# A gated recurrence and a two-layer network on one core: wide first products in the opening, two banks for the last halves, and a new order

## The chip, the cores and the metric

The kernel runs on one core of a Trainium2 chip. A core has five engines that work side by side, each on its own list of instructions: TensorE (PE; its weight loads are listed apart as PEld), VectorE (DVE), ScalarE (ACT), GpSimd (POOL) and SyncE (SP), which issues DMAs. The metric is the device time of one execution in microseconds (us). The kernel before takes 181.42 us, the median of three runs (181.39 to 182.42).

## The reference

Inputs are `q`, `k`, `v` and `f_logit`, each of shape (4 batches, 8 heads, 768 steps, 48), and two weight matrices, 384 x 2048 and 2048 x 384, all float32. What is computed:

```python
f = 1.0 / (1.0 + np.exp(-f_logit))
for t in range(S):
    state = f[:, :, t, :, None] * state + np.einsum('bhd,bhe->bhde', k[:, :, t], v[:, :, t])
    y[:, :, t] = np.einsum('bhd,bhde->bhe', q[:, :, t], state)
x = y.transpose(0, 2, 1, 3).reshape(B * S, H * D)
h = x @ w_in
out = (h * (1.0 / (1.0 + np.exp(-h)))) @ w_out
```

The output is 3072 tokens x 384, float32.

## The kernel before, in words

**Tiling.** The 768 steps of each batch are cut into 6 chunks of 128. A (batch, chunk) is a unit; two units make a pair, and there are 12 pairs, numbered 0 to 11. Pairs 0 to 3 (form "T") hold chunks 0 and 1 of one batch; their rows are loaded interleaved, two steps to a partition. Pairs 4 to 11 (form "N") hold one chunk of two batches. A name such as `ki.3.1` is operation `ki` of pair 3, unit 1.

**What is done for a unit.**

- `f`, `k`, `q`, `v`: loads, issued by SP (L241), for a whole pair or (`f.0.0`, `f.0.1`; `v.4.1` and the like) a half of it.
- `E`, `L`: ACT makes exp(-f) (L248) and log(1 + that) (L260, L263).
- `cs`: PE sums the logarithms along the steps with a triangular matrix (L324, L331) and gives the totals (L328, L334).
- `ia`, `a`, `al`: ACT takes exponentials of the sums (L336) and of the totals (L278, L338).
- `ki`, `qg`: DVE or POOL multiply `k` and `q` with these (L341).
- `tq`, `qkc`: PE transposes both (L348) and ACT or DVE copy the result; or `qkD`, a DMA transpose from SP, in place of both. A copy on ACT or DVE is a helper's line, L185 or L187.
- `sc`: PE makes the scores of the chunk (L369 for T, L373 for N), into two PSUM banks; `at`: DVE multiplies them with a mask (L377).
- `vb`: `v` in bf16 (a copy on ACT, DVE or POOL).
- `y`, `yi`: PE makes the output of the recurrence from scores (L285, L389) and from the state before (L385); `d`: PE makes what the chunk adds to the state (L297, L406); `sd`, `su`: DVE or POOL update the state (L410, L420).
- `yc`, then `yT` and `xc`: the output is copied as bf16, transposed by PE (L397) and copied to `xT`; or `yD`, a DMA transpose (L401).

**The two-layer network, by pairs.** `mi.P.j` is the first product for double block j, 0 to 7: 256 of the 2048 hidden columns. It has 2 column blocks x 3 parts of the sum, six matrix products (L271), each with its own weight load; the moving side is `xT` of both units, 256 columns. `mi.P.j.i`, with a third number, does it for unit i alone, with 128 columns and six products again. `si.P.j` (ACT, L276) takes SiLU of both units at once, from the PSUM bank to `hT`. `mo.P.i.h` is a quarter of the second product of a unit (four matrix products of 384 columns, L306); four of them, h = 0 to 3, add up in one PSUM bank. `oc` copies that bank (ACT or DVE), `so` writes it out (SP or POOL, L316 and L318). In pair 11 the second product is cut once more, `mo.11.i.h.half`, each half with 192 columns, and so are `oc` and `so`.

**Weights.** `wi.0` to `wi.3` load a quarter of `w_in` each (two double blocks: `wi.2` holds double blocks 4 and 5), `wo.0` to `wo.3` a quarter of `w_out`. POOL issues them (L216, L219), with a cast to bf16.

**What sets the order.** The order is written out by hand: `PLAN` is one list of words `operation:engine:buffers`. The engine letter is P, A (ACT), V (DVE), G (POOL) or S (SP). Each engine runs its own words in the list's order, and the tile framework adds the waits. The last field is the buffer that the result gets: for PE a PSUM bank 0 to 7, so an operation waits until the bank's last reader is done. `idle.512.n` is n products on zeros (L465). The first four loads of the list are issued ahead of all else. Where ACT goes over from exponentials to SiLU or back, it loads a table (L513).

In before's list the first products of pairs 0 and 1 are all in single units (`mi.0.2.0` ... `mi.1.6.1`), those of pairs 2 to 11 are for both units.

Of the kernel before, what the change touches and what calls it, by code (L numbers as in the profile page):

```python
# [41 lines left out]
tq.1.0:P:2 q.3.0:S:3 a.2.0:A:3 qg.1.1:G: sc.0.0:P:3,4 qkc.1.0:A:1 sc.0.1:P:6,7 at.0.0.1:V:0 k.3.0:S:3 wi.1:G: at.0.0.0:V: E.3.0:A:1 idle.512.2::5
tq.1.1:P:5 at.0.1.0:V:1 wi.2:G: d.1:P:1,4 qkc.1.1:A: v.2.0:S:2 su.1.0:V:0 wi.0:G: at.0.1.1:V: al.2:A:2 L.3.0:A:0 idle.512.3::2 sc.1.0:P:2,3 ki.2.0:G:4
sc.1.1:P:6,1 at.1.0.1:V:2 vb.0.0:A:2 cs.3.1:P:5 vb.0.1:A:3 at.1.1.0:V:3 qg.2.0:G: al.3:A:3 ia.2.1:A:2 d.0:P:7,3 at.1.1.1:V: a.2.1:A:0 cs.3.0:P:6
ia.3.1:A:4 su.0.0:V:0 qg.2.1:G:2 y.0:P:0,1 a.3.0:A:1 at.1.0.0:V: yc.0.0:A:0 yi.0.1:P: tq.2.0:P:7 a.3.1:A:3 wi.3:G: yc.0.1:V:1 ia.3.0:A:0 y.1:P:0,2
# [4 lines left out]
mi.0.1.1:P:0 si.0.3:A:1 mi.0.1.0:P: mi.0.5.1:P: si.1.5:A: ki.3.0:G: mi.0.0.0:P:6 si.0.1:A: mi.0.6.0:P:5 mi.0.0.1:P: su.1.1:G:0 mi.0.7.1:P:4 si.0.0:A:  # L50
mi.0.7.0:P: si.0.2:A: mi.0.6.1:P: ki.3.1:G: mi.1.1.0:P: si.0.6:A: mi.1.7.0:P:0 tq.3.0:P:6 mi.1.7.1:P: qkc.3.0:A:1 mi.0.4.0:P:2 tq.3.1:P:5 si.1.7:A:
mi.0.4.1:P: f.4.0:S:1 mo.0.0.0:P:6 qkc.3.1:A: mo.0.1.0:P:0 si.1.1:A: mi.1.6.1:P:5 si.0.5:A: mi.1.6.0:P: si.1.2:A: mo.1.1.0:P:7 si.1.6:A: mo.0.1.1:P:
si.0.4:A: si.0.7:A: sc.3.1:P:3,1 sc.3.0:P:5,2 at.3.1.0:V:2 vb.2.0:A:4 mo.0.1.2:P: at.3.1.1:V: mo.1.1.1:P: at.3.0.0:V:3 mo.0.0.1:P: q.4.0:S:4
mo.0.1.3:P: vb.3.0:V:5 mo.1.1.2:P: vb.3.1:V:6 oc.0.1:V:0 mo.1.1.3:P: at.3.0.1:V: v.5.0:S:4 mo.0.0.2:P: vb.2.1:V:2 v.5.1:S: oc.1.1:V:1 d.2:P:4,3
so.1.1:G: y.2:P:1,5 su.2.0:V:0 v.4.0:S:5 d.3:P:0,2 E.4.0:A:0 sd.2.1:V:0 y.3:P:7,4 yc.3.0:V:1 yi.2.1:P: mo.1.0.0:P:3 L.4.0:A:1 yc.2.1:V:2 yT.3.0:P:7
su.3.0:V:0 mo.1.0.1:P: yc.2.0:V:0 v.8.1:S:0 mo.0.0.3:P: sd.3.1:V:1 yT.2.1:P:5 oc.0.0:A:2 cs.4.0:P:0 k.4.0:S:4 xc.2.1:V:2 yi.3.1:P: a.4.0:A:2 so.0.0:G:
mo.1.0.2:P: ia.4.0:A:1 q.4.1:S: xc.3.0:A:3 yT.2.0:P:1 mo.1.0.3:P: xc.2.0:V: E.5.0:A:1 k.6.1:S:5 mi.2.2:P:2 al.4.0:A:4 cs.4.1:P:6 mi.2.3:P:5 al.4.1:A:5
a.4.1:A:3 q.5.0:S:5 L.5.0:A:2 mi.2.7:P:7 k.5.1:S:0 yc.3.1:A:1 mi.2.4:P:1 ia.4.1:A:0 ki.4.0:G:1 q.5.1:S: mi.2.5:P:0 oc.1.0:A:3 vb.4.0:G:3 yT.3.1:P:4
mi.2.0:P:6 xc.3.1:V: su.2.1:G:0 mi.3.6:P:3 si.2.3:A:2 mi.3.1:P:4 qg.4.0:V: si.2.7:A: k.4.1:S: su.3.1:G:0 si.2.5:A: mi.3.7:P:5 si.3.1:A:3 f.6.0:S:2
mi.2.6:P:7 vb.5.1:A:0 si.3.7:A: d.4.0:P:0 v.4.1:S: mi.2.1:P:4 sd.4.0:V:0 si.2.6:A: qg.4.1:V:2 tq.4.0:P:5 si.2.4:A: mi.3.2:P:0 si.2.1:A: k.7.0:S:1  # L60
si.2.0:A: mi.3.0:P:7 ki.4.1:G: qkc.4.0:A:0 cs.5.1:P:1 mi.3.5:P:4 qkD.4.1:S:1 si.3.0:A: mo.2.1.0:P:6 si.2.2:A: si.3.5:A: sc.4.0:P:5,7 v.7.0:S:1
# [485 lines left out]
```

## Time and profile before

| | us |
|---|---|
| median of three runs | 181.42 |
| the profiled execution | 180.93 |
| its span, first to last instruction | 179.2 |
| PE busy | 170.5 |
| PE weight loads busy | 129.0 |
| ACT busy | 132.7 |
| DVE busy | 79.7 |
| POOL busy | 61.6 |

The profiled execution took 180.93 us, of which 179.2 lie between its first and its last instruction. The granted TensorE clock was full in all 40 slices of the page. A row of a timeline reads: start, length, engine, line and operation, output <- inputs, how many, and in brackets the idle time of the engine ahead of it with what ended it. In the chain of waits a row has start, length, and what the time went to. A row of the list of waits has the instruction, what it waited for, the total in us, how often, and the longest. Matrix products overlap, so that the length of one row is longer than what it adds to the next row's start.

### The profile page before, as it was taken

To read this page: it belongs to the slowest core of one execution; us is meant where nothing else is said; L and a number is where in the kernel's file an instruction comes from. 1 tells how busy PE (TensorE), PEld (TensorE's weight loads), DVE (VectorE), ACT (ScalarE), POOL (GpSimd) and SP (SyncE) were. 2 spreads that over 40 slices of the span, in tenths; PEclk is the share of its full clock that TensorE was granted. 3 is DMA by queue.
4 is the path that set the end of the run, shared out by engine and by line. 5 is a ranking of instruction groups with operands and counts; after the bars stand their busy time and mean duration, and the time that the engine had idled before them with its cause. 6 is when DMAs were issued, how large, how long until landed. Compare 5 with 4: busy or idle time off the path is not lost.

```text
span 179.2 us, 4981 instructions
## 1 busy us (share of the span) xinstructions
PE 170.5 (95%) x2042; PEld 129.0 (72%) x2044; DVE 79.7 (44%) x166; ACT 132.7 (74%) x251; POOL 61.6 (34%) x106
## 2 busy tenths in 40 slices
PE   6769989999999999999999999999999999999993
PEld 2345779975788866778678877875876786788782
DVE  7078994008821246456673703342335747500002
ACT  3989983895289999999967558988796991178410
POOL 6036995000274004554044170636303592000010
PEclk9999999999999999999999999999999999999999
DMA  6999999999999799998478998994994496320043
GB/s 159 324 325 325 240 204 207 199 187 190 242 230 212 92 208 221 168 241 144 84 145 170 188 210 141 252 263 103 179 251 94 97 190 215 88 70 0 0 150 117
DMA packets 109366, 31.91 MB, mean 178 GB/s; under 512 B 103536, under 2 KB 108768, under 8 KB 109344
## 3 DMA queue, kind: packets, MB, share of 16 engines
q1 hardware_dynamic: 104464, 25.60, 70.2%
q0 software_dynamic: 4880, 6.00, 15.7%
q8 instruction: 16, 0.26, 0.6%
q14 instruction: 6, 0.05, 0.1%
HBM read 25.17 MB, written 4.72 MB: 167 GB/s over the span
## 4 chain that ended last, share of the span: by engine, by line
PE 77%; ACT 9%; DVE 4%; DMA 3%; SPq 2%; issue 1%; POOL 1%; DVEq 0%
PE pb L306 32%; PE pb L271 32%; ACT hT L276 4%; DMA q<-in_q_dram 3%; PE pb L373 2%; SPq L241 2%; PE pb L385 2%; PE pb L348 2%; PE pb L389 2%; DVE qk L341 2%; ACT L513 1%; DVE atm L377 1%; PE pb L331 1%; PE pb L397 1%; DVE st L420 1%
## 5 line engine op out<-in xcount | busy, mean ns | idle before, releaser
L306 PE MATMUL pb<-w_out_sb,hT 128*128 128x384 bf16 (+1 forms) x416 | 70.4, 314 | 0.2 <-ACT hT L276 0.2
L271 PE MATMUL pb<-xT,w_in_sb 128*128 128x256 bf16 (+1 forms) x672 | 68.9, 257 | 0.0
L271 PEld LDWEIGHTS <-w_in_sb 128*128 128x128 bf16 x672 | 56.6, 98 | 7.5 <-issue 0.3
L276 ACT ACTIVATE hT<-pb 128x512 bf16<-128x512 f32 x96 | 51.8, 617 | 12.4 <-PE pb L271 12.0
L306 PEld LDWEIGHTS <-hT 128*128 128x128 bf16 x416 | 37.7, 98 | 18.7 <-ACT hT L276 0.4
L377 DVE TENSOR_TENSOR atm<-pb,triu 128x512 bf16<-128x512 f32 x32 | 20.6, 684 | 20.5 <-PE pb L373 17.8
L336 ACT ACTIVATE x<-pb 128x384 f32<-128x384 f32 x48 | 22.1, 508 | 1.5 <-PE pb L331 1.4
L420 POOL TENSOR_TENSOR st<-sd,al 48x192 bf16<-48x192 f32 x32 | 16.6, 518 | 18.7 <-PE pb L385 12.1
L341 POOL TENSOR_TENSOR qk<-q,x 128x384 bf16<-128x384 f32 x11 | 11.3, 1025 | 31.9 <-ACT x L336 14.5
L513 ACT ACT_TABLE_LOAD x15 | 19.2, 1283 | 0.3
L185 ACT COPY ob<-pb 128x384 f32<-128x384 f32 (+1 forms) x15 | 6.8, 453 | 12.6 <-PE pb L306 12.6
L377 DVE TENSOR_TENSOR atm<-pb,mask 128x512 bf16<-128x512 f32 x16 | 10.2, 685 | 12.4 <-ACT hT L276 11.1
L187 DVE COPY ob<-pb 128x384 f32<-128x384 f32 (+1 forms) x11 | 5.8, 535 | 22.2 <-PE pb L306 22.2
L318 POOL DMA_DIRECT2D out_dram<-ob x8 | 4.6, 578 | 28.4 <-ACT ob L185 24.8
L316 POOL DMA_DIRECT2D out_dram<-ob x14 | 7.6, 548 | 19.6 <-DVE ob L187 15.9
L341 DVE TENSOR_TENSOR qk<-q,x 128x384 bf16<-128x384 f32 x13 | 7.6, 593 | 13.7 <-ACT x L336 13.7
L248 ACT ACTIVATE e<-f 128x768 f32<-128x768 f32 (+1 forms) x13 | 10.4, 800 | 4.4 <-DMA f<-in_f_logit_dram 4.2
L410 DVE TENSOR_TENSOR sd<-pb,st 128x384 f32<-128x384 f32 x16 | 8.9, 554 | 10.6 <-PE pb L406 3.9
L341 POOL TENSOR_TENSOR qk<-k,x 128x384 bf16<-128x384 f32 x10 | 10.8, 1082 | 6.4 <-ACT al L278 2.0
L185 ACT CAST yb<-pb 128x384 bf16<-128x384 f32 x12 | 5.6, 479 | 9.7 <-PE pb L389 9.6
L341 DVE TENSOR_TENSOR qk<-k,x 128x384 bf16<-128x384 f32 x14 | 9.9, 710 | 0.9 <-ACT x L336 0.9
L187 DVE CAST yb<-pb 128x384 bf16<-128x384 f32 x12 | 6.6, 556 | 8.0 <-PE pb L389 5.9
(72 smaller groups left out, 157.4 us busy)
## 6 DMA issues: line engine op xcount, KB each, us to landing
f<-in_f_logit_dram SPq DMA_DIRECT2D x11, 384.0 KB, 4.7
q<-in_q_dram SPq DMA_DIRECT2D x16, 192.0 KB, 4.1
v<-in_v_dram SPq DMA_DIRECT2D x16, 192.0 KB, 3.9
k<-in_k_dram SPq DMA_DIRECT2D x16, 192.0 KB, 3.9
k<-in_k_dram SPq DMA_DIRECT2D x4, 384.0 KB, 4.8
v<-in_v_dram SPq DMA_DIRECT2D x4, 384.0 KB, 9.5
q<-in_q_dram SPq DMA_DIRECT2D x4, 384.0 KB, 4.9
w_in_sb<-in_moe_w_in_dram POOLq DMA_DIRECT2D x4, 384.0 KB, 9.5
```

The costliest lines, as they stand in the source:

```text
L185: nc.scalar.copy(dst, src)
L187: ENG[eng].tensor_copy(dst, src)
L248: return nc.scalar.activation(e, at("f", P)[:, j * w:(j + 1) * w], AF.Exp, scale=-1.0)
L271: nc.tensor.matmul(h[:, i, cols], w_in_sb[:, kk, n * 128:(n + 1) * 128], at("xT", P)[:, kk, cols], start=(kk == 0), stop=(kk == KT - 1))
L276: return nc.scalar.activation(at("hT", P)[:, 2 * j:2 * j + 2, :], at("h", P, j).rearrange("p (n c) -> p n c", n=2), AF.Silu)
L306: nc.tensor.matmul(at("o", P, i)[:, cols], at("hT", P)[:, n, i * C:(i + 1) * C], w_out_sb[:, n, cols], start=(n == 0), stop=(n == NT - 1))
L336: nc.scalar.activation(at(kind, P, i).rearrange("p h d -> p (h d)"), at("cs", P, i)[:, 0:HD], AF.Exp, scale=1.0 if kind == "ia" else -1.0)
L341: ENG[eng].tensor_mul(at("qk", P, i)[:, j, :, 0:D], heads("qk"[j], P, i), at("ia" if j else "a", P, i))
L377: ENG[eng].tensor_mul(at("atm", P, i)[:, r], at(f"s{r}", P, i).rearrange("p (n c) -> p n c", c=C), mask[:, None, :].to_broadcast([C, NP, C]))
L410: nc.vector.tensor_add(at("sd", P, i), d_ps, prev_state(P, i))
L420: ENG[eng].tensor_mul(at("st", P, i)[lo:lo + D, :, r * D:(r + 1) * D], src[lo:lo + D, :, r * D:(r + 1) * D], al_of(P, i)[lo:lo + D, :, Non ...
L513: nc.scalar.preload_act_table_set(TABLES[mode])
```

## The change

Four things change, all but the third in the list.

1. For pairs 0 and 1, double blocks 0, 1, 4, 5, 6 and 7 take the first product for both units at once (`mi.0.4`, as in the later pairs). Double blocks 2 and 3 stay in single units.
2. The list is in a new order throughout. The opening now begins with `f` of pairs 0, 1 and 2; before it began with `f.2`, `k.0` and `f.0`. Some operations change their engine: `qkc` from ACT to DVE (four), `vb` from ACT and DVE to POOL (ten), `ki` and `qg` from DVE to POOL (four each), `xc` from ACT to DVE (three), five `so` from POOL to SP. There are 16 tables loaded in both. The `idle` products are 24 ahead of the first `mi` in both, in other portions.
3. In the code, the output of a half of pair 11 gets a PSUM bank of its own: both `mo` and `oc` look the bank up under the half's name. Before, both halves of a unit shared one.
4. Of the last writes, `so.11.0.0` stays on POOL but comes near the end of the list, behind the last `mo`; before, ten `mo` words still followed it.

PE has 144 instructions fewer: 72 products with their weight loads.

```diff
-f.2.0:S:0 k.0.0:S:0 f.0.1:S:1 f.0.0:S: E.2.0:A:0 f.1.0:S:2 L.2.0:A:0 v.1.0:S:0 q.0.0:S:0 idle.512.11::0 cs.2.1:P:0 E.0.1:A:1 E.0.0:A: k.1.0:S:1
...
-wo.0:G: ki.2.1:V: yc.1.0:A:2 yT.0.0:P:5 sd.0.1:V:0 yi.1.1:P: yT.0.1:P:1 yc.1.1:A:0 tq.2.1:P:6 xc.0.0:V:0 wo.1:G: xc.0.1:A: qkc.2.0:V:0 v.3.0:S:3
-yT.1.0:P:0 yT.1.1:P:3 xc.1.0:A:1 mi.0.2.0:P:2 qkc.2.1:V: su.0.1:G:0 xc.1.1:A: mi.0.3.0:P:5 mi.1.3.0:P:1 sd.1.1:V:1 mi.1.3.1:P: qg.3.0:V:3 wo.2:G:
-mi.0.2.1:P: sc.2.1:P:7,0 si.1.3:A:0 wo.3:G: qg.3.1:V:0 sc.2.0:P:3,6 at.2.1.1:V:0 mi.1.5.1:P:4 mi.1.2.1:P:1 at.2.0.0:V:1 mi.1.2.0:P: at.2.0.1:V:
...
-so.11.1.1:S: oc.11.0.1:A: so.11.0.1:S:
+f.0.1:S:0 f.0.0:S: f.1.0:S:1 f.2.0:S:2 q.0.0:S:0 E.0.0:A:0 q.1.0:S:1 E.0.1:A: L.0.0:A:0 L.0.1:A: k.0.0:S:0 idle.512.11::0 cs.0.0:P:0 cs.0.1:P:1
+ia.0.0:A:0 k.1.0:S:1 E.1.0:A:1 E.2.0:A:0 f.3.0:S:3 a.0.0:A:1 L.2.0:A:1 qg.0.0:G:0 q.2.0:S:2 L.1.0:A:2 idle.512.5::2 cs.2.1:P:2 cs.2.0:P:3 a.0.1:A:2
+ki.0.0:V: v.1.0:S:0 cs.1.1:P:4 ia.0.1:A:3 qg.0.1:V:1 a.2.0:A:4 tq.0.0:P:5 ki.0.1:V: ia.2.1:A:1 v.0.0:S:1 cs.1.0:P:6 qkc.0.0:V:0 a.1.0:A:0 tq.0.1:P:7
+a.1.1:A:2 qg.1.0:V:2 ia.1.0:A:3 k.2.0:S:2 qkc.0.1:V: qg.1.1:G:3 ia.1.1:A:0 al.1:A:0 idle.512.4::0 sc.0.0:P:0,5 ki.1.0:V: q.3.0:S:3 a.2.1:A:2
+at.0.0.1:V:0 ki.1.1:G: E.3.0:A:0 idle.512.1::6 tq.1.0:P:6 at.0.0.0:V: vb.1.1:A:0 k.3.0:S:3 wi.2:G: tq.1.1:P:7 qkc.1.0:A:1 wi.1:G: vb.1.0:V:1
+qkc.1.1:V: sc.0.1:P:4,5 v.2.0:S:2 L.3.0:A:0 at.0.1.1:V:1 qg.2.1:G:4 al.0:A:1 at.0.1.0:V: idle.512.3::0 cs.3.0:P:0 v.3.0:S:3 ia.3.0:A:3 sc.1.0:P:6,7
+wi.0:G: ia.2.0:A:0 d.1:P:5,1 al.2:A:2 vb.0.1:A:2 wi.3:G: vb.0.0:V:3 at.1.0.1:V:2 sc.1.1:P:4,3 at.1.0.0:V: a.3.0:A:2 d.0:P:2,7 at.1.1.1:V:3 ki.2.1:G:
+y.0:P:6,0 at.1.1.0:V: yc.0.0:A:0 cs.3.1:P:3 qg.2.0:G:2 su.0.0:V:0 ia.3.1:A:1 y.1:P:6,4 su.1.0:V:0 ki.2.0:G: yc.1.0:A:1 yi.0.1:P: yT.0.0:P:2 f.4.0:S:0
+yc.0.1:A:2 yi.1.1:P: tq.2.1:P:5 yc.1.1:A:0 wo.0:G: yT.0.1:P:6 yT.1.0:P:0 xc.0.1:V:0 tq.2.0:P:4 xc.0.0:V: wo.1:G: yT.1.1:P:6 qkc.2.0:V:0 mi.0.4:P:2
+xc.1.1:A:1 xc.1.0:A: qkc.2.1:V: mi.0.5:P:6 al.3:A:3 a.3.1:A:4 sd.1.1:V:0 mi.1.5:P:4 qg.3.1:G:3 mi.0.2.1:P:0 mi.1.4:P:5 wo.2:G: si.0.5:A:0 si.1.5:A:1
+sc.2.0:P:3,1 ki.3.0:G:0 at.2.0.0:V:0 mi.1.3.0:P:6 mi.0.2.0:P: sd.0.1:V:1 mi.0.1:P:4 wo.3:G: si.0.2:A: q.4.0:S:4 at.2.0.1:V: mi.1.0:P:3 qg.3.0:G:
...
+mo.11.1.3.0:P: oc.11.1.1:A:3 mo.11.0.3.0:P: oc.11.1.0:V: so.11.1.1:S: mo.11.0.2.1:P: oc.11.0.0:V:0 so.11.1.0:S: mo.11.0.3.1:P: so.11.0.0:G:
+oc.11.0.1:A: so.11.0.1:S:
...
-                nc.tensor.matmul(at("o", P, i)[:, cols], at("hT", P)[:, n, i * C:(i + 1) * C], w_out_sb[:, n, cols], start=(n == 0), stop=(n == NT - 1))
+                nc.tensor.matmul(at("o", P, i, *rest[3:])[:, cols], at("hT", P)[:, n, i * C:(i + 1) * C], w_out_sb[:, n, cols], start=(n == 0), stop=(n == NT - 1))
...
-            copy(eng, at("ob", P, i)[:, cols], at("o", P, i)[:, cols])
+            copy(eng, at("ob", P, i)[:, cols], at("o", P, i, *rest[2:])[:, cols])
...
-            return [("o", *rest[:2])]
+            return [("o", *rest[:2], *rest[3:])]
```

More of the change, by code (lines that the diff above doesn't have):

```diff
@@ L42 @@
[L42 to L45, printed above, removed]
@@ L50 @@
[L50 to L53, printed above, removed]
@@ L54 @@
[L54 to L61, printed above, removed]
@@ new lines @@
+vb.3.0:G:5 tq.3.0:P:7 qkc.3.1:V:1 si.1.7:A: su.0.1:G:0 mo.0.1.0:P:0 si.1.2:A: qkc.3.0:V: mo.0.1.1:P: sc.2.1:P:3,5 sc.3.0:P:1,6 sc.3.1:P:2,7
+at.3.0.0:V:1 mo.1.1.1:P: at.2.1.1:V:2 mo.1.1.2:P: at.3.0.1:V: f.5.0:S:1 mo.0.1.2:P: at.2.1.0:V: q.4.1:S: mo.0.0.0:P:1 vb.2.1:V:6 at.3.1.0:V:3
+mo.0.1.3:P: vb.2.0:V:2 mo.1.1.3:P: E.4.0:A:1 k.4.0:S:4 mo.0.0.1:P: oc.1.1:A:0 L.4.0:A:1 so.1.1:G: y.2:P:5,6 d.2:P:3,2 oc.0.1:A:1 su.2.0:V:0
+mo.0.0.2:P: v.8.1:S:4 at.3.1.1:V: cs.4.0:P:4 mo.0.0.3:P: ia.4.0:A:0 sd.2.1:V:1 yc.2.0:V:2 k.5.1:S:5 d.3:P:0,3 E.5.0:A:0 y.3:P:7,2 su.3.0:V:0 q.5.0:S:5
@@ new lines @@
+L.8.0:A:2 mi.4.7:P:1 qg.6.1:V:3 so.2.0:G: ia.6.1:A:2 mo.3.0.2:P: sd.5.1:V:0 a.7.0:A:1 qkD.5.0:S:3 al.6.0:A:4 mi.4.3:P:3 a.6.0:A:0 qg.7.0:G:2
+mi.4.0:P:2 qg.6.0:G:1 sc.5.1:P:7,6 si.4.0:A:0 at.5.1.0:V:1 mo.3.0.3:P: ki.6.0:G: si.4.7:A: v.7.1:S: at.5.1.1:V: mi.4.1:P:0 q.7.1:S: sd.5.0:V:1
+mi.4.4:P:2 ki.6.1:V: q.9.0:S:2 tq.6.0:P:7 si.4.4:A: mi.4.2:P:1 qkc.6.0:A:0 k.7.1:S: y.5.1:P:6 si.4.2:A: mi.4.5:P:4 yc.5.1:V:2 su.5.1:G:0 si.4.1:A:
+v.9.1:S:2 sc.5.0:P:2,7 si.4.5:A: sc.6.0:P:1,6 at.5.0.0:V:3 vb.6.1:G:3 mo.4.0.0:P:0 k.8.0:S: oc.3.0:A:2 at.5.0.1:V: si.4.3:A: cs.8.0:P:4 mi.4.6:P:2
```

93 lines of the change are left out of this document (46 added, 47 removed).

## The prediction

> **What bounds the kernel now.** I read the page first, then PE's own waits, then the chain of waits.
>
> ```profile
> PE 170.5 (95%) x2042; PEld 129.0 (72%) x2044; DVE 79.7 (44%) x166; ACT 132.7 (74%) x251; POOL 61.6 (34%) x106
> ...
> PE 77%; ACT 9%; DVE 4%; DMA 3%; SPq 2%; issue 1%; POOL 1%; DVEq 0%
> ```
>
> PE is busy for 95% of the span and carries 77% of the chain that ended last. Busy time is modelled, so the list of what PE waited for decides:
>
> ```profile
> PE pb L324 <- ACT lf L260: 1.9, 3, 0.8
> PE pb L465 <- POOL triu masks.py:66: 1.4, 1, 1.4
> PE pb L369 <- issue: 0.9, 1, 0.9
> PE pb L348 <- DVE qk L341: 0.4, 1, 0.4
> PE pb L348 <- POOL qk L341: 0.4, 1, 0.4
> PE pb L306 <- ACT hT L276: 0.2, 1, 0.2
> ```
>
> Five of the six lie in the opening or just behind it; the last, 0.2 us, is the only one in the long stretch of products. The timeline of PE gives the stretch its ends:
>
> ```profile
> 23.58 1.84 PE L271 MATMUL pb<-xT,w_in_sb 128*128 128x128 bf16 x30
> 25.35 0.52 PE L369 MATMUL pb<-qkTT 48*64 48x128 bf16 x21
> 26.72 0.36 PE L369 MATMUL pb<-qkTT 48*64 48x128 bf16 x11 [0.85 <-issue]
> ...
> 166.51 9.66 PE L306 MATMUL pb<-w_out_sb,hT 128*128 128x384 bf16 x88
> ```
>
> The first product (L271) starts at 23.58 and the last (L306) ends at 166.51 + 9.66 = 176.17. Between them lie 152.6 us in which PE runs dry once for long, 0.85 us in the middle of the score products L369, with no engine as the releaser ("issue"). So the time is three terms: the start of the first product, PE's own work behind it, and the tail. ACT comes near to it for a while, as the view by windows shows:
>
> ```profile
> 80.00:90.00 10.00, 10.00 (x127) 7.61 (x123) 7.02 (x13) 9.94 (x22) 2.82 (x4) 1.00 0.64 116
> ```
>
> In these ten us (busy time of PE, PEld, DVE, ACT, POOL in this order) ACT has 9.94 and PE 10.00: ACT is the second bound, there alone.
>
> **The change part by part.** *Fewer, wider products.* Twelve double blocks (six of each of pairs 0 and 1) change from two halves of six 128-column products to one set of six with 256 columns. The chain of waits has the price of each:
>
> ```profile
> 35.00 0.67 PE pb L271 x12
> ...
> 115.94 1.31 PE pb L271 x12
> ```
>
> Twelve products take 0.67 us at 128 columns and 1.31 us at 256, so a double block costs 0.67 us in halves and 0.655 whole. Twelve of them: **-0.2 us**. The weight load in front of each product is hidden in both forms; the gain is not the halved count of products.
>
> *The stall of 0.85 us.* Its place in the stream is the 22nd of 32 score products, each with a weight load ahead of it, behind 60 instructions of half-width products (30, each with its weight load) that cover 1.77 us. The page's list of DMA queues has one that carries instructions:
>
> ```profile
> q8 instruction: 16, 0.26, 0.6%
> ```
>
> That is 16 packets of 16 KB. 0.26 MB over PE's 2042 + 2044 instructions is 64 bytes each, 256 to a block, so PE ate a block faster than a loaded DMA system brought the next. In the new order the same place in the stream (60 instructions behind the first product, then scores) holds four whole double blocks and one half, 2.96 us instead of 1.77, then 16 score products instead of 32, then products again. The block has at least 1.3 us more to arrive than before, and it was 0.85 late: **-0.85 us** (from 0, if the stall is something else, to -0.85). [...]
>
> *The start of the first product.* 24 idle products stand ahead of it in both versions, as do all real ones, so only the dependences matter. Rows to walk with, from the chain of waits and the timelines of ACT, DVE and POOL:
>
> ```profile
> 5.24 4.81 DMA q<-in_q_dram
> ```
> ```profile
> 4.05 0.84 ACT L248 ACTIVATE e<-f 128x768 f32<-128x768 f32 x1 [2.03 <-DMA f<-in_f_logit_dram]
> ...
> 9.57 1.24 ACT L336 ACTIVATE x<-pb 128x384 f32<-128x384 f32 x3
> ...
> 24.51 1.28 ACT L513 ACT_TABLE_LOAD   x1
> 25.80 0.60 ACT L276 ACTIVATE hT<-pb 128x512 bf16<-128x512 f32 x1
> ```
> ```profile
> 10.62 0.55 DVE L341 TENSOR_TENSOR qk<-k,x 128x384 bf16<-128x384 f32 x1
> ...
> 11.56 1.36 DVE L341 TENSOR_TENSOR qk<-k,x 128x384 bf16<-128x384 f32 x1
> 12.84 0.68 DVE L187 COPY qkTT<-pb 128x1024 bf16<-128x1024 bf16 x1
> ...
> 17.87 2.48 DVE L377 TENSOR_TENSOR atm<-pb,mask 128x512 bf16<-128x512 f32 x4
> 20.27 0.71 DVE L420 TENSOR_TENSOR st<-pb,al 48x192 bf16<-48x192 f32 x2
> ...
> 23.02 0.35 DVE L187 COPY xT<-pb 128x384 bf16<-128x384 bf16 x1
> ```
> ```profile
> 14.89 1.00 POOL L341 TENSOR_TENSOR qk<-q,x 128x384 bf16<-128x384 f32 x1 [2.39 <-ACT x L336]
> 15.83 2.46 POOL L216 DMA_DIRECT2D w_in_sb<-in_moe_w_in_dram  x3
> ```
>
> The first load lands at 4.05, the sixth at 5.24 + 4.81 = 10.05: 1.2 us a load. New order: f of pairs 0, 1, 2, q of 0 and 1, then k.0 sixth (10.05), k.1 seventh (11.25), v.1 tenth (14.9), v.0 (16.1). ACT: both halves of E and L of pair 0 to 5.8, ia.0.0 at 6.4 behind the cumulative sums, two E, a.0.0, two L to 10.3, then the exponentials at 0.41 (1.24 / 3). ki.0.0 waits for k.0 until 10.1, takes 0.55; its transpose stands on PE ahead of cs.1.0, which runs at 11.4, so a.1.0 comes at 11.95 and ia.1.1 ends at 13.65. On DVE qkc.0.1 ends at 13.65, and ki.1.0 meets qg.1.1 on POOL (1.0): the row at 11.56 shows such a meeting, 1.36 in place of 0.55, so it ends near 14.4. Scores of unit 0 start at 14.15 behind four idle products. DVE then has four masks, two of vb, qkc.1.1 (0.68), with short waits, and from 18.2 four masks at 0.62 (2.48 / 4) to 20.75; su.0.0 and su.1.0 (0.71 each) to 22.05; on PE yi.1.1, tq.2.1, yT.0.1 to 22.9; xc.0.1 and xc.0.0 at 0.35 to 23.75. mi.0.4 needs both units and starts at **23.8: +0.2 us** (-1.0 to +1.5: the meeting and the short waits of the walk all gone, or two more meetings at 0.8).
>
> *Just behind it.* si.0.5 must empty bank 6 before mi.1.3.0: xc.1.1, xc.1.0, al.3 and a.3.1 end ACT's exponentials at 25.3, the table load (1.28) and si.0.5 (0.60) at 27.2; PE is there at 27.1, and all of PE's work waits behind it: +0.15. The weights of the first product, from the view of their tile, all four quarters and then the fourth alone:
>
> ```profile
> DMA to landing us min/median/max: 7.4/9.5/11.0
> ```
> ```profile
> DMA to landing us min/median/max: 9.9/9.9/9.9
> ```
>
> The first quarter was issued at 15.83 and landed 7.4 later (the shortest of the four), at 23.2, just ahead of the product; the fourth was issued at 21.26 and landed 9.9 later, at 31.1: 2.65 us from quarter to quarter. Now the first issue stands behind ki.1.1 on POOL, near 15.3, so quarters land at 22.7, 25.4, 28.0 and 30.7; PE wants them at 23.8, 25.8, 28.1 and 30.7. It just fits; if landings stay at 23.2 + 2.65 each, the third is 0.5 late. I take **+0.3 us** for both (0 to +1.2).
>
> *The banks of the last halves and the tail.* The products of the halves are L306, and the whole wait of L306 is 0.2 us, so a second bank frees no time: 0. What moves is the last copies and writes. By line, POOL's last write before, SP's last three, POOL's 14 writes of line 316, and a last copy on DVE:
>
> ```profile
> L318 POOL DMA_DIRECT2D out_dram<-ob x1: 545/545/545, 172.2 to 172.2; - x1
> ...
> DMA to landing us min/median/max: 2.9/2.9/2.9
> ```
> ```profile
> L318 SPq DMA_DIRECT2D out_dram<-ob x3: 332/332/332, 175.5 to 176.6; - x3
> ...
> DMA to landing us min/median/max: 1.6/1.6/1.9
> ```
> ```profile
> DMA to landing us min/median/max: 2.4/3.7/5.0
> ```
> ```profile
> 175.61 0.36 DVE L187 COPY ob<-pb 128x192 f32<-128x192 f32 x1 [0.16 <-PE pb L306]
> ```
>
> Before, POOL's write left at 172.2, four us ahead of the end; SP's last left at 176.6, landed 1.6 later, and the span ended 3.0 us behind PE. Now so.11.0.0 on POOL waits for DVE's second copy (0.36 each; the first starts 0.9 ahead of PE's end), and nothing stands behind it on POOL. It leaves 0.1 ahead of PE's end E and, at 2.9, lands at E + 2.8, where SP's last lands at E + 2.0. **+0.8 us** (+0.3 to +2.9 with the 2.4 and 5.0 of POOL's other writes, which left while loads ran). [...] The rows say 1.3 apart and I go by them.
>
> *Work that changes engine.* ACT gives up four qkc, four vb, three xc; POOL takes four ki, four qg, ten vb; five writes go from POOL to SP. I cost all at nothing: PE's products cover them, ACT's full stretch gets lighter, POOL was 34% busy. Without the cover each ki or qg on POOL costs 0.45 more than on DVE (1.00 for 0.55), 3.6 us for the eight. On SP the moved writes stand behind copies made long before; so.7.0 has loads of pairs 10 and 11 right behind it, wanted some ten us later. f.4 now runs ahead of f.5; where that may show is the second rival.
>
> **Sum.** +0.2 - 0.2 - 0.85 + 0.3 + 0.8 = +0.25 against the profiled execution's 180.93 (179.2 of span and 1.7 around it), which is 0.5 under the median 181.42. On the median: **181.7**, no change that a measurement of this kernel can tell (about 1%).
>
> **The rivals.**
> 1. *The stall stays or moves*: it is no late block, or another block is late elsewhere. The term of -0.85 falls: 182.5. For it: nothing in the trace names what PE waited for. Against it: the byte count, and the place, where PE takes its instructions fastest. [...]
> 2. *Slower: pair 4's gate load is late.* cs.4.0 stands on PE 22.1 us of products behind the first, at 46.2. It needs f.4 landed, E (0.84), one output copy, L (0.84): 2.2 us with its waits, so it decides from a landing at 44.0. f.4 is the 17th load, as f.5 was; the view of tile f at that load, and POOL's timeline:
>
> ```profile
> L241 SPq DMA_DIRECT2D f<-in_f_logit_dram x1: 6882/6882/6882, 19.9 to 19.9; - x1
> ...
> DMA to landing us min/median/max: 22.9/22.9/22.9
> ```
> ```profile
> 24.65 1.54 POOL L219 DMA_DIRECT2D w_out_sb<-in_moe_w_out_dram  x2
> ```
>
> issued at 19.9, landed 22.9 later, 42.8, held up by the weights. The last two weight issues, at 24.65 and 0.8 later, now stand behind qg.3.1 (which waits for a.3.1 at 25.3) and ki.3.0 on POOL: 26.3 and 28.1, 1.7 and 2.7 us later. If loads slip by these 2.7 us to 45.5, cs.4.0 waits 1.5, and the loads of pairs 4 and 5 behind it about 1 more: 184.2. Against it: weight landings were 2.7 apart with issues far ahead, so a later issue need not show.
> 3. *Faster.* The opening's short waits all go (-1.0 at the start in place of +0.2), none comes just behind it, and POOL's write lands in 2.4: 179.7; with L306's 0.2 gone too, 179.5. For it: ACT has six operations fewer ahead of the first product (35 for 41). Against it: the walk is set by loads, by PE's order and by DVE, not by ACT.
> 4. *Nothing of what it says*: whole blocks at 0.655 gain only 0.2, as above; this is in the forecast.
>
> **How the numbers follow.** Forecast 0.58 (all within 1%), rival 1 0.13 (0.10 within, 0.03 slower), rival 2 0.17 (slower), rival 3 0.12 (0.07 faster, 0.05 within). Faster by over 1% (under 179.6): 0.07; within: 0.73; slower (over 183.2): 0.20. The range 179.8 to 184.0 leaves out half of rival 3 and the upper half of rival 2; it takes in each term's bounds one or two at a time, not all on one side.
>
> **What would show it.** First L271 at 23.3 to 25, at 256 columns; no idle of "issue" at L369; the twelve blocks' products at 109 ns; POOL's last write issued within 0.3 us of PE's end and its landing ending the span, 3.5 to 4 us behind PE. Wrong: a PE wait at L331 or L324 near 46 us, a wait of PE for POOL's qk in pairs 4 to 7, or a tail of 3.0.

## The result, and the profile after

The changed kernel takes 184.19 us (median of four runs, 183.82 to 184.61), the kernel before 181.54 beside it: ratio 1.0138, 95% interval [1.0105, 1.0171]. **It is 1.4% slower**; the forecast was 181.7, the range to 184.0. The profiled execution took 184.28 with a span of 182.5. Single executions of one kernel here spread by up to 2.5 us, so below a version's time is given as a ratio to the kernel before, timed beside it, and a profile's own time is named where it lies far off. A version is called by the first part of its label, e1 to e17; what was expected of it stands in front of its result.

Line numbers are one lower than before (L270 is the first product, L305 the second). The page of the changed kernel, its busy time, the granted clock by slices, the bytes moved by slices and the chain:

```profile
PE 171.6 (94%) x1972; PEld 128.3 (70%) x1972; DVE 75.8 (42%) x159; ACT 127.5 (70%) x240; POOL 69.7 (38%) x117
...
PEclk9987999999999999999999999999999999999999
...
GB/s 140 284 277 287 248 206 205 205 197 183 241 167 214 170 226 189 152 190 171 188 107 197 192 149 214 183 194 163 206 173 97 174 212 151 66 108 47 0 125 91
...
PE 48%; issue 19%; DMA 11%; ACT 8%; POOL 6%; DVE 5%; SPq 1%; POOLq 0%; ACTq 0%
```

PE's busy time is 1.1 us more though 144 instructions went. The clock, full before, dips in the third and fourth slice (9 to 18 us), and the loads of the second and third slice run at 284 and 277 GB/s; in the kernel before these slices have 324 and 325:

```profile
GB/s 159 324 325 325 240 204 207 199 187 190 242 230 212 92 208 221 168 241 144 84 145 170 188 210 141 252 263 103 179 251 94 97 190 215 88 70 0 0 150 117
```

The chain's shares can't be set beside those of before: it now goes back from POOL's end, and its 19% "issue" is POOL with nothing to do.

What PE waited for in the changed kernel (total, times, longest):

```profile
PE pb L323 <- ACT lf L259: 2.5, 2, 2.0
PE pb L464 <- POOL triu masks.py:66: 1.4, 1, 1.4
PE pb L347 <- DVE qk L340: 1.1, 1, 1.1
PE pb L405 <- POOL vb L186: 0.7, 1, 0.7
PE pb L270 <- DMA xT<-yb: 0.5, 1, 0.5
PE pb L384 <- DVE st L419: 0.3, 1, 0.3
```

The "issue" of 0.85 is gone. Larger waits for `lf` and `qk` stand in the opening, and a wait for POOL's `vb` (L405), here in d.5.1 at 74.8 us. PE's timeline:

```profile
9.93 0.48 PE L323 MATMUL pb<-lf,tincl 128*128 128x384 bf16 x2 [2.00 <-ACT lf L259]
...
12.80 0.61 PE L347 MATMUL pb<-ident,qk 128*128 128x128 bf16 x4 [1.11 <-DVE qk L340]
...
16.23 0.42 PE L368 MATMUL pb<-qkTT 48*64 48x128 bf16 x16
...
26.55 3.12 PE L270 MATMUL pb<-xT,w_in_sb 128*128 128x256 bf16 x30
29.59 0.42 PE L368 MATMUL pb<-qkTT 48*64 48x128 bf16 x16
29.94 7.76 PE L270 MATMUL pb<-xT,w_in_sb 128*128 128x128 bf16 x90
...
47.74 0.33 PE L330 MATMUL pb<-lf,triu 128*128 128x384 bf16 x1
...
171.59 7.05 PE L305 MATMUL pb<-w_out_sb,hT 128*128 128x384 bf16 x68
```

The first product starts at 26.55, the last ends at 178.64. So of the three terms of the prediction the start is **+2.97** (23.58 before), the stretch of products 152.1 us instead of 152.6, **-0.5**, and the tail 3.87 instead of 2.99, **+0.87**: together the 3.35 us by which the span grew.

The late start begins with late loads. The two issues of `k` (tile `k`) in the changed kernel:

```profile
L240 SPq DMA_DIRECT2D k<-in_k_dram x2: 1150/1150/1151, 6.6 to 7.8; - x2
...
DMA to landing us min/median/max: 5.5/5.5/5.5
```

Issued at 6.6, k.0 landed 5.5 later, at 12.1; the prediction's walk had 10.05. After PE's two idle stretches of 2.0 and 1.1 us its clock is granted at about half (windows of two us; the figure of the clock is the third from the end):

```profile
12.00:14.00 2.00, 1.20 (x8) 0.87 (x9) 1.82 (x4) 0.13 (x1) 0.00 (x0) 0.61 1.10 300
14.00:16.00 2.00, 2.00 (x13) 1.15 (x10) 1.67 (x4) 1.71 (x5) 0.97 (x2) 0.54 0.98 259
```

### The profile page after: what moved, and what is told of

Its sections match the earlier page's. It is cut to its first block, busy times and chain, and to the rows that moved or that the text cites. A ratio compares the mean times of both kernels' runs of the same rounds, so it can differ in the third digit from the quotient of the medians.

```text
span 182.5 us, 4858 instructions
## 1 busy us (share of the span) xinstructions
PE 171.6 (94%) x1972; PEld 128.3 (70%) x1972; DVE 75.8 (42%) x159; ACT 127.5 (70%) x240; POOL 69.7 (38%) x117
## 4 chain that ended last, share of the span: by engine, by line
PE 48%; issue 19%; DMA 11%; ACT 8%; POOL 6%; DVE 5%; SPq 1%; POOLq 0%; ACTq 0%
PE pb L305 19%; PE pb L270 18%; DMA w_out_sb<-in_moe_w_out_dram 7%; DMA f<-in_f_logit_dram 3%; POOL qk L340 3%; DVE atm L376 2%; ACT x L335 2%; ACT hT L275 2%; PE pb L347 2%; PE pb L372 1%; PE pb L384 1%; POOL st L419 1%; PE pb L388 1%; ACT e L247 1%; POOL vb L186 1%
## 5 line engine op out<-in xcount | busy, mean ns | idle before, releaser
L305 PE MATMUL pb<-w_out_sb,hT 128*128 128x384 bf16 (+1 forms) x416 | 71.2, 314 | 0.1
L270 PE MATMUL pb<-xT,w_in_sb 128*128 128x256 bf16 (+1 forms) x600 | 68.3, 268 | 0.6 <-DMA xT<-yb 0.5
L270 PEld LDWEIGHTS <-w_in_sb 128*128 128x128 bf16 x600 | 55.6, 97 | 8.9 <-issue 0.7
L305 PEld LDWEIGHTS <-hT 128*128 128x128 bf16 x416 | 37.2, 97 | 18.4 <-issue 0.4
L340 POOL TENSOR_TENSOR qk<-q,x 128x384 bf16<-128x384 f32 x15 | 14.9, 997 | 27.5 <-ACT x L335 19.3
L340 POOL TENSOR_TENSOR qk<-k,x 128x384 bf16<-128x384 f32 x14 | 14.3, 1020 | 15.1 <-issue 6.8
L317 POOL DMA_DIRECT2D out_dram<-ob x5 | 2.9, 573 | 27.9 <-DVE ob L186 27.9
L186 POOL CAST vb<-v 128x384 bf16<-128x384 f32 x15 | 7.3, 505 | 12.5 <-DMA v<-in_v_dram 12.2
L340 DVE TENSOR_TENSOR qk<-k,x 128x384 bf16<-128x384 f32 x10 | 6.6, 659 | 10.5 <-ACT x L335 10.5
L464 PE MATMUL pb<-zero,triu 128*128 128x512 bf16 x24 | 8.7, 512 | 1.4 <-POOL triu masks.py:66 1.4
```

What stands on the lines that cost most here:

```text
L186: ENG[eng].tensor_copy(dst, src)
L270: nc.tensor.matmul(h[:, i, cols], w_in_sb[:, kk, n * 128:(n + 1) * 128], at("xT", P)[:, kk, cols], start=(kk == 0), stop=(kk == KT - 1))
L305: nc.tensor.matmul(at("o", P, i, *rest[3:])[:, cols], at("hT", P)[:, n, i * C:(i + 1) * C], w_out_sb[:, n, cols], start=(n == 0), stop=(n ...
L340: ENG[eng].tensor_mul(at("qk", P, i)[:, j, :, 0:D], heads("qk"[j], P, i), at("ia" if j else "a", P, i))
```

## The experiments

### The tail

```diff
-so.11.0.0:G:
+so.11.0.0:S:
```

> The changed kernel with one word changed: so.11.0.0 is issued by SP and not by POOL. The prediction's term: POOL's write lands 2.9 us after its issue and so ends the span; without it the span ends 3.0 us behind PE's last product and not 3.85, -0.8 us, about 183.4. What the profile of the changed kernel says instead: POOL's write landed after 2.0 us, ahead of SP's last, and what came late was POOL's own closing drain, 1.0 us behind that landing, with the closing barrier behind it; then the end comes 0.5 to 0.6 us sooner, the last landing stays where it is (2.3 us behind PE), about 183.6. Rival: the tail is set by SP's four writes in a row and nothing is gained, 184.2. The opening is word for word that of the changed kernel, so this is a second look at it: if the late loads of the opening (k.0 at 12.1 instead of the 10.05 that the walk had) belong to this order of loads, k.0 lands at 11.5 to 12.5 here too; if they were an accident of one execution, it lands near 10.05 and the first product starts near 24.

Ratio 1.0056 [1.0018, 1.0094]: 0.8% under the changed kernel. The tail has 0.75 us of it in the profile, half of the 0.8%; where the other half comes from isn't shown. PE's last product and the page's span of this run:

```profile
170.93 7.05 PE L305 MATMUL pb<-w_out_sb,hT 128*128 128x384 bf16 x68
```
```profile
span 181.1 us, 4856 instructions
```

177.98 to 181.1 is a tail of 3.1 against 3.87. What made it, in the changed kernel (POOL's write; then POOL's closing drains) and in the kernel before (the drains):

```profile
L317 POOL DMA_DIRECT2D out_dram<-ob x1: 542/542/542, 178.7 to 178.7; - x1
...
DMA to landing us min/median/max: 2.0/2.0/2.0
```
```profile
L541 POOLq DRAIN  x3: 46/93/3022, 178.7 to 182.2; - x3
```
```profile
L542 POOLq DRAIN  x3: 46/102/4199, 172.2 to 178.9; - x3
```

POOL's write landed 2.0 us after its issue, at 180.74, ahead of SP's last (180.96). But a drain of 3.0 us follows it on POOL, from 178.7 to 181.73, and the closing barrier waits for it. Before, the drain of 4.2 us ran from 172.2 and was over at 176.4. By its size (0.75) the run doesn't choose between the two theories of the expectation; the order of the ends does, and it is that of the second. From the last landing to the end of the span it is 1.55 us in the changed kernel and 0.97 in e1, as in the kernel before (0.98): the drain is worth 0.57 us, and the rest is that the last landing itself comes 2.1 us behind PE in e1 and not 2.3. k.0 landed at 11.8 here: the late loads came again.

### The late loads

```diff
-q.1.0:S:1 ... k.0.0:S:0        (e2: the two change places)
+k.0.0:S:0 ... q.1.0:S:1
-f.0.1:S:0 f.0.0:S: f.1.0:S:1   (e5: k.0 first of all)
+k.0.0:S:0 f.0.1:S:0 f.0.0:S: f.1.0:S:1
```

Of e2:

> The changed kernel with k.0 loaded ahead of q.1 (they change places; nothing else moves). Theory of the late load: k.0 lands one load, 1.2 us, sooner, near 10.9; the wait of PE for qk at the first transpose goes, cs.1.0 behind it runs 1.1 to 1.3 us sooner, a.1.0 and qg.1.1 with it, and the first product starts 1.0 to 1.4 us sooner, near 25.3: 182.9. Rival, the rest of the opening is the bound (DVE's row of masks, copies and states, or POOL's meeting with DVE): the first product moves by less than 0.4 us, 184.

Of e5:

> The changed kernel with k.0 loaded first of all, ahead of the two halves of f.0; f.1, f.2, q.0 and q.1 follow as they were. In the traces so far the third load, f.1, landed at 6.4 to 6.6 in every order that begins with the two halves (5.2 by 1.2 us a load), and DMA packets of over 60 ns were 40 to 62 in the first 16 us, where the kernel before and its wide version had 13 and 16. Theory A: a half load first empties the queue before the third load's packets are there, and the packets of later loads stay out of step. Then with a whole load first the long packets fall under 25, f.1 lands near 6.4 though a whole load now stands ahead of it, f.2 near 7.6, k.1 near 11.3, v.1 near 15 and v.0 near 16.2; scores of unit 0 start near 14, the first product near 24.3, and the time is near 182.0. Rival B: it is loads of one tensor in a row (f, f, f, then q, q) that stall each other: the long packets stay above 40, f.1 lands at 7.2 or later, and the first product starts at 26 or later: 184.

k.0 ahead of q.1: ratio 1.0137 [1.0086, 1.0189], nothing gained. PE's timeline there:

```profile
13.87 0.42 PE L368 MATMUL pb<-qkTT 48*64 48x128 bf16 x16 [0.46 <-DVE qkTT L186]
...
19.13 0.32 PE L323 MATMUL pb<-lf,tincl 128*128 128x384 bf16 x1 [2.22 <-ACT lf L259]
...
26.14 2.12 PE L270 MATMUL pb<-xT,w_in_sb 128*128 128x256 bf16 x18
```

k.0 landed at 10.09, and the first scores (L368) start at 13.87: the walk's 14.15 for a k.0 at 10.05 was sound. But v.1, at 16.9 for the walk's 14.9, held ACT's copy and with it `lf` of pair 3 (2.22 us); behind that wait the granted clock was half from 19.4 to 22.9, and the first product came 0.4 us sooner only. It isn't one late load, it is the stream. k.0 first of all: 1.0133 [1.0077, 1.0189]; the gap ahead of f.1 shrank to 0.3 us, but later loads lagged (q.1 at 11.6), and f.2, a load later, held PE's sums of pair 2 to 11.1. The first product starts at 25.77 there. Neither theory of that expectation held whole.

```diff
-f.0.1 f.0.0 f.1 f.2 q.0 q.1 k.0 k.1 f.3 q.2 v.1        (e6)
+f.0.1 f.0.0 q.0 f.1 k.0 f.2 q.1 k.1 f.3 v.1 q.2
-f.0.1 f.0.0 f.1 f.2 q.0 q.1 k.0 k.1 f.3 q.2 v.1 v.0 k.2   (e11; e12 the same, from + to -, in the kernel before)
+f.2 k.0 f.0.1 f.0.0 f.1 v.1 q.0 k.1 q.1 f.3 v.0 k.2 q.2
```

Of e6:

> The changed kernel with the first loads in turns: halves of f.0, q.0, f.1, k.0, f.2, q.1, k.1, f.3, v.1, q.2. A look at the stream of loads, for the two theories of the run with k.0 first. B (loads of one tensor in a row stall each other): long packets under 25 in the first 16 us, the third load lands near 5.3 and the sixth near 8.9. A (halves first): the third load lands at 6.4 or later again, and the long packets stay above 40. The time isn't the question: f.2 comes a load later, which holds PE's sums of pair 2 and all behind them about 1 us; 182.5 to 185.

Of e7, the kernel before once more:

> The kernel before, unchanged, for a second profile of it on this chip: how much of the late loads goes with the order of the list and how much with the execution. If with the order: landings as before (k.0 5.2, q.0 10.05, v.0 14.9), under 20 long packets, first product at 23.6, the stall of 0.85 us in the score products at the same instruction. If with the chip or the execution: 40 or more long packets and the first product at 24.5 or later.

Of e11:

> The changed kernel with its first 13 loads in the order of the kernel before (f.2, k.0, f.0, f.1, v.1, q.0, k.1, q.1, f.3, v.0, k.2, q.2); all engines' work as in the changed list. A look at the stream of loads: in four profiles of the kernel before and its variants DMA packets of over 60 ns numbered 13 to 22 in the first 16 us, in six of the changed kernel and its variants 40 to 63. If the order of the loads makes the long packets: under 25 of them, and the loads land about 1.2 us apart (thirteenth near 17.5). If the other engines' work makes them: 40 or more, the thirteenth load at 19 or later. First product between 24 and 27 in either case.

Of e12:

> The mirror image: the kernel before with its first 13 loads in the changed order, all engines' work as before. If the order of the loads makes the long packets: 40 or more of them in the first 16 us and the thirteenth load at 19 or later; if the other engines' work makes them: under 25, the thirteenth at 17.5 to 18.5. The start of the first product will be late in either case, since v.1 and f.2 come later than the list's work wants them: 25 to 27.5.

A long packet is here a DMA packet of over 60 ns in the first 16 us, counted in the trace. All four of these runs are one profile each. In e6, with the loads in turns, there are 63 long packets and the third load lands at 6.1, so it isn't the neighbours of one tensor. The kernel before, profiled again in an execution of 183.63 (e7), had 22 long packets, the stall (0.76) at the same instruction and its first product at 24.74, so an execution adds lateness of its own, about 1.2 us in that one. The mirror pair decides: the changed kernel with before's order of loads (e11) has 13 long packets, the kernel before with the changed order (e12) 57. **What happens at the head of the queue follows the order of the loads**, not the work of the engines. The time doesn't follow the long packets alone: e11 took 184.55 and e12 187.55, with the first product at 27.87 and 29.73, both later than expected, since each list's work wants its data in its own order (PE waits 2.3 us in e11 and 3.3 us in e12 for one `lf`). The view by windows, 2.5 to 5.5 us (the last figure is GB/s), for the kernel before, the changed kernel, e11, e12 and e14:

```profile
2.50:5.50 3.00, 3.00 (x9) 1.10 (x8) 1.70 (x13) 1.42 (x2) 1.15 (x6) 1.00 1.14 317
```
```profile
2.50:5.50 3.00, 3.00 (x8) 1.05 (x7) 1.70 (x13) 1.48 (x4) 1.14 (x6) 1.00 1.05 273
```
```profile
2.50:5.50 3.00, 3.00 (x8) 1.03 (x7) 1.70 (x13) 0.00 (x0) 1.14 (x6) 1.00 1.14 315
```
```profile
2.50:5.50 3.00, 3.00 (x8) 1.03 (x7) 1.70 (x13) 0.00 (x0) 1.15 (x6) 1.00 1.00 245
```
```profile
2.50:5.50 3.00, 3.00 (x9) 1.08 (x8) 1.69 (x13) 1.14 (x2) 1.14 (x6) 1.00 1.14 316
```

Of nineteen profiles, the seven whose list begins with the two halves of f.0 moved 245 to 273 GB/s in these three us, the twelve that begin with a whole load 299 to 317. That left one edit to make:

```diff
-f.0.1:S:0 f.0.0:S: ... E.0.0:A:0 ... E.0.1:A: L.0.0:A:0 L.0.1:A:
+f.0.0:S:0 ... E.0.0:A:0 ... L.0.0:A:0
```

> The changed kernel with f.0 loaded by one DMA instead of two halves, and its E and L each as one operation. In every profile of an order that begins with the two halves the third load landed at 6.1 to 6.6 (0.65 to 1.3 us more than 1.2 behind the second); in every one that begins with a whole load there was no such gap. Theory: the gap is the halves'. Then f.1 lands at 5.3 to 5.6 and not at 6.5, f.2 at 6.6 to 6.9, k.0 at 10.2 to 10.8 and not at 11.4 to 12.1; the first product starts 1.0 to 1.5 us sooner, at 25.0 to 25.5: 182.7 to 183.2. Rival: the gap belongs to what follows (three loads of f in a row), f.1 lands at 6.4 again, and the time stays at 184.2.

Ratio **0.9996 [0.9972, 1.0020]**: level with the kernel before, so the whole loss of 1.4% is gone, about twice what was expected. (The changed kernel itself was not timed again beside e14.) Making E and L one operation each is not what gains: L of pair 0 ends at 6.04 in e14 and at 5.78 in the changed kernel. f.1 landed at 5.44, f.2 at 6.63, k.0 at 10.65. Where the second half of the gain comes from isn't shown. The mean granted clock was 0.997 or more in eight of ten runs (in three of four of the changed kernel 0.989 to 0.991), but the changed kernel's one run at full clock still took 183.82, so the clock alone doesn't make it. The profiled run of e14 was one of the other two (183.66; first product 25.49; clock at half from 18.7 to 22.1), so the profile shows the gain badly and the median (181.70) shows it.

### The clock

```diff
-idle.512.5::2 cs.2.1:P:2 ... tq.0.0:P:5
+idle.512.14::2 cs.2.1:P:2 ... idle.512.4::5 tq.0.0:P:5
```

> The changed kernel with 9 more idle products in PE's gap at 7.9 to 9.9 us and 4 more in the one at 11.7 to 12.8, so that PE isn't idle there. Theory of the clock: the granted clock of 0.61 and 0.54 at 12 to 16 us follows PE's two idle stretches; with them filled it stays at 1.0, the transposes and sums at 12.8 to 14.9 take about 1.2 us instead of 2.1, and the first product starts 0.3 to 0.8 us sooner: 183.4 to 183.9. Rival: the products on zeros stand in front of work that would have been ready, and the start stays or comes up to 0.5 us later: 184.2 to 184.7.

Ratio 1.0075 [1.0047, 1.0102], first product at 25.71, 0.84 sooner. The loads were as late (f.1 6.4, k.0 11.8). The same two windows:

```profile
12.00:14.00 2.00, 1.89 (x21) 1.28 (x20) 2.00 (x5) 0.76 (x2) 0.00 (x0) 1.00 1.14 312
14.00:16.00 2.00, 1.60 (x28) 0.91 (x26) 2.00 (x4) 1.71 (x6) 1.81 (x2) 1.00 1.05 276
```

Full clock in both. In the changed kernel PE's idle gaps cost twice: the wait (2.0 and 1.1 us), then slow products behind it (a clock of 0.61 and 0.54 in these windows). Not every gap does: in e5 PE sat idle for 1.2 us from 6.2 and for 1.5 us from 9.5, and its clock stayed full.

### Do the repairs add up?

```diff
 (e10: the idle products of e3 and the word of e1; e15: these and e14's edit; e17: as e15 without idle.512.4::5)
```

Of e10:

> The changed kernel with both repairs that gained by themselves: 13 more idle products in PE's two gaps (first product 0.84 us sooner) and so.11.0.0 on SP (tail 0.76 shorter). If they add up: 1.6 us under the changed kernel, ratio to the kernel before near 1.005, first product near 25.7, tail 3.1. What is left over the kernel before, near 0.8 us, would then be the late loads. Rival: the tail's gain was one of chance, and the ratio stays at 1.0075 as with the idle products alone.

Of e15:

> The changed kernel with all three repairs: f.0 whole, 13 more idle products in PE's gaps, so.11.0.0 on SP. If they add up: first product at 24.3 to 24.9, tail 3.1, no dip of the granted clock, 181.3 to 181.8, ratio to the kernel before 0.998 to 1.002; the whole loss of the change would then be accounted for. Rival: with the loads in time the idle products stand in the way of ready work, and it is no faster than the two repairs without f.0 whole, 1.006.

Of e17:

> The changed kernel with f.0 whole, so.11.0.0 on SP, and only the first 9 of the 13 idle products, those in the gap that ended at 9.9. With all 13 and the loads in time, the 4 others stood from 11.24 to 12.1 ahead of the first transposes, whose input was ready. If nothing else bounds the opening: first scores at 13.9 to 14.0 instead of 14.81, first product at 24.5 instead of 25.43, stretch 150.7 to 151.2, tail 3.1: 180.4 to 180.9, 0.4 to 0.8% under the kernel before. Rival: what follows (ACT's L.3.0 ahead of the sums of pair 3, DVE's row of masks and copies) is the bound, as in the run with f.0 whole alone, where scores started at 13.97 and the first product at 25.49: then it stays at 181.5.

Idle products and tail together (e10): 1.0059 [1.0037, 1.0082]. That fits the sum, but the rival's 1.0075 lies in the interval too; only the tail of its profile (3.11; an execution of 183.58) speaks for the sum. All three (e15): 0.9979 [0.9953, 1.0005], as expected, though its first product starts at 25.43, later than the 24.3 to 24.9 expected. It is level with f.0 whole alone within the intervals: the idle products add nothing that shows, and the 0.7 us by which its tail is shorter (3.17 for 3.86 in e14) is too little for these intervals to tell. With nine idle products only (e17): 0.9976 [0.9946, 1.0005]; 0.4% under before at least was expected, 0.2% came; its stretch of products took 151.9 for the 150.7 to 151.2 expected. Its profile shows the opening with loads in time and full clock, PE's first scores and first product, and DVE:

```profile
14.03 0.42 PE L368 MATMUL pb<-qkTT 48*64 48x128 bf16 x16 [0.46 <-DVE qkTT L186]
...
24.66 1.58 PE L270 MATMUL pb<-xT,w_in_sb 128*128 128x256 bf16 x13
```
```profile
15.78 1.09 DVE L186 CAST vb<-v 128x384 bf16<-128x384 f32 x1
...
19.03 2.46 DVE L376 TENSOR_TENSOR atm<-pb,mask 128x512 bf16<-128x512 f32 x4
21.42 1.47 DVE L419 TENSOR_TENSOR st<-pb,al 48x192 bf16<-48x192 f32 x4
```

The scores start 0.1 ahead of the walk, the product at 24.66, 0.86 behind it: DVE's copy of `vb` took 1.09 us (the next one 0.52), and the row of four masks starts at 19.03 for the walk's 18.2. Why that copy was slow is not shown: POOL was issuing weight loads beside both copies.

### The wide products, and the stall

```diff
-mi.0.4.0:P:2 ... mi.0.4.1:P:     (e4, e16: so for twelve double blocks, at the second word's place)
+mi.0.4:P:2
-idle.512.11::0                   (e8)
+idle.512.1::0 idle.256.20::0
```

Of e4:

> The kernel before with part 1 of the change alone: the twelve double blocks of pairs 0 and 1 taken whole, each at the place of its second half; order, loads and tail as before. By the prediction's term 12 times 0.015 us, -0.2 us: 181.3, the first product at 23.6, and the stall of 0.85 us in the middle of the score products stays, since nothing ahead of it changes. Rival: fewer instructions also move the later instruction blocks or banks are held for longer, a gain or loss of 0.5 to 1.5 us that shows as a wait of PE at L271, L276 or L306 behind 30 us.

Of e16, the same kernel:

> Part 1 alone once more, with more rounds, beside the version with the opening of the kernel before and the rest of the changed list. -0.2 us, ratio 0.999, if whole blocks are worth 0.015 us each; its first profile had a stall of issue of 1.9 us in the score products in place of 0.85, in a late execution (loads to 0.6 us late, clock 0.99), so this also shows whether the stall is longer with it: then the ratio is 1.000 to 1.005.

Of e8:

> The kernel before with ten of the eleven idle products of 512 columns at its start as twenty of 256 columns: the same columns, but ten products and ten weight loads more ahead of all of PE's work. Theory of the instruction block: the 0.85 us stall stands at a block's edge, every 256 instructions of PE, so it moves 20 instructions, ten score products, up: from behind the 21st to behind the 11th, with 0.5 to 1.0 us of issue. Rival, something at that place of the work (a bank, a wait that the profile doesn't name): it stays behind the 21st. In either case the time stays within 0.4 us of before.

In the kernel before, part 1 alone gives 0.9989 [0.9949, 1.0029], then 0.9966 [0.9942, 0.9990]: only the second shows a gain, and -0.2 us (0.999) lies at the edge of its interval. The stall stays, at the same place, 1.0 us long in the second profile (1.9 in the first, which took 183.0). With ten products and ten loads more ahead, e8 has it here:

```profile
25.60 0.36 PE L369 MATMUL pb<-qkTT 48*64 48x128 bf16 x11
27.26 0.49 PE L369 MATMUL pb<-qkTT 48*64 48x128 bf16 x21 [1.30 <-issue]
```

Behind the 11th score product and no longer behind the 21st, exactly the 20 instructions, and 1.30 long. It stands at a place in the count of PE's instructions, not in the work. The run took 181.67.

The packets of the instruction queue in the traces tie it to the fetch. In the six profiles with the stall (before, e4, e7, e8, e12, e16) PE's wait ends 1.3 to 1.5 us behind the end of the second 16 KB packet: in the kernel before the packet ends at 25.4 and the wait at 26.7. In the thirteen without it PE gets to the same place in its stream, about the 704th recorded instruction, 1.6 us or more behind the packet's end: in the changed kernel the packet ends at 27.1, and PE is there at 30.2.

### The rest of the new order

```diff
 (e9: before's list up to its first mi, then the changed list; so.11.0.0 on SP)
 (e13: as e9, and)
-wi.1:G: ... wi.2:G:
+wi.2:G: ... wi.1:G:
```

Of e9:

> The changed kernel with the opening of the kernel before: all of before's list up to its first product (its loads, idle products, sums, transposes, scores), then the changed list from mi.0.4 on, buffers renumbered to fit; and so.11.0.0 on SP. Theory: what costs is the new opening and POOL's last write alone, and the rest of the new order is 0.5 to 1.5 us shorter than before's. Then the first product starts as in the kernel before, 23.6 to 24.9, the stretch from there to PE's last product takes 151.5 to 152.2 (152.6 and more before), the tail 3.0, and the time is 0.5 to 1.2 us under the kernel before's. Rival: the rest of the new order needs its own opening (ACT, DVE and POOL stand otherwise at the first product); new waits of PE behind 24 us give the gain back, and the time is that of the kernel before or up to 1 us over it. The stall of issue: the place in PE's stream is 2 instructions from that of the changed kernel, so none is expected at L368.

Of e13:

> As the run with the opening of the kernel before, but wi.2 is issued ahead of wi.1: there the first product, mi.0.4, waited 1.9 us for wi.2, which before's opening issues second (landing 27.1), while the quarter issued first had landed at 24.5. If that wait is the whole of what kept it from gaining: the first product starts 1.9 to 2.6 us sooner, at 23.6 to 24.9, the stretch stays at 151.5 to 152.5, the tail at 3.0 to 3.1, and the time is 1.0 to 1.5 us under the kernel before's: near 180.2. Rival: a later quarter (wi.1 for block 2, wi.0 for blocks 0 and 1) is now late in its turn and gives 0.5 to 1.5 us back, or the stall of issue comes; then it is level with the kernel before.

e9: 1.0054 [1.0030, 1.0078]; its rival held. PE's longest wait in its profile, an execution of 184.56 where the median is 182.15:

```profile
PE pb L270 <- DMA w_in_sb<-in_moe_w_in_dram: 1.9, 1, 1.9
```

The changed list begins with double block 4, and before's opening issues that quarter (wi.2) second. With the two quarters exchanged, e13 is at 0.9986 [0.9954, 1.0018]: level with the kernel before and with e16. So the new order behind the first product, and the second bank for the halves with it, has no gain that shows beyond the wide products'; the 1.0 to 1.5 us expected did not come. Why not is open: e13's profile took 182.64 and doesn't show the median's execution. The second bank was not tried by itself.

## Why the prediction was wrong, point by point

- **The start of the first product (+0.2, bounds -1.0 to +1.5): the step that failed.** It measured +2.97. Its sentence "The first load lands at 4.05, the sixth at 5.24 + 4.81 = 10.05: 1.2 us a load" was read from an order that begins with a whole load and carried over to one that begins with two halves; there the two halves land by 4.0 to 4.2, as forecast, but f.1 lands at 6.4 to 6.6 instead of 5.25 in six profiles of six that begin with halves and then f.1. The second sentence, "24 idle products stand ahead of it in both versions, as do all real ones, so only the dependences matter", left out where they stand: PE, idle for 2.0 us at 7.9 and for 1.1 us at 11.7, ran at half its clock from 12.4 to 15.9. By the profiles, one execution each, e17 takes both away and starts at 24.66: of the 2.97 they are 1.89 (0.84 of it by e3's idle products alone, while loads are late), and 1.08 is the new opening's own length, inside the bounds and 0.86 over the value taken; one slow copy of DVE (1.09 us for 0.52) is 0.57 of that.
- **Wider products (-0.2):** right in sign; e16 has 0.1 to 0.6% of gain, e4 none that shows.
- **The stall (-0.85):** right, and by its mechanism: it is gone in the changed kernel, e8 shows that it hangs on the count of instructions (20 more ahead, 20 instructions up), and the packets tie it to the fetch (in six profiles of six it ends 1.3 to 1.5 us behind the second packet). The 256 instructions to a block are an estimate from the pages, counting PE's instructions alone: 4086 on 16 packets before, 3944 on 15 in the changed kernel, 255 and 263 each; no run shows a block's length by itself. The stall shows as 0.76 to 1.9 us in six profiles.
- **Just behind it (+0.3):** no such wait came; PE's timeline has no idle from 26.55 to 37.7 (the rows at 26.55, 29.59 and 29.94). But the start was 3 us late, which gave the weights time. In e17, with the start at 24.66, PE does wait 0.26 us at 29.16 for the third quarter of `w_in`, the one that the prediction feared for.
- **Work that changes engine (0):** wrong by a little. (The counts of the change are net: DVE gives POOL eight `ki` and seven `qg` and takes four and three back.) The 0.7 for POOL's `vb` is vb.5.1, one of those moved; 0.6 in e1, none in e15 and e17. In e14's profile PE also waits 0.9 us for POOL's `qk` at 64.4. The stretch came to -0.5 where the terms gave -0.75, and partly by luck: the waits of over 0.1 us in it add up to 1.2 us (0.73 and 0.49) for 1.0 before, so losing the stall gained nothing net. The products without waits take 0.7 us less; the wide blocks were to give 0.2 of that, and the rest is open.
- **The tail (+0.8):** right in size, +0.87, by luck, since the mechanism was another: not the landing at 2.9 but POOL's drain behind it (0.57) and SP's last landing (0.3 later behind PE than before). POOL's landing itself took 2.0 us against 1.9 for SP's neighbour. The rows of before that the term was read from, 2.9 and 1.6, were 1.3 apart; this pair of writes is 0.1 apart.
- **The second rival** gave the time (184.2) by luck, and not the reason. f.4 landed late, as it said, past its 44.0:

```profile
L240 SPq DMA_DIRECT2D f<-in_f_logit_dram x1: 9128/9128/9128, 23.0 to 23.0; - x1
...
DMA to landing us min/median/max: 22.2/22.2/22.2
```

  at 45.2. But the first sums of pair 4 (L330) run at 47.74 without a wait, since the first product, from which their place was counted, was itself 3 us late.
